# A wider pitch for the rows of X2, two buffers for the k = 0 products, one for the copies of x3, and a new order table

## The chip, the cores and the metric

The kernel runs on one core of a Trainium2 chip. The metric is device time in microseconds (us) of one execution. Times before are the median of three runs; the traces are of one profiled execution. PE is the matrix engine, DVE the vector engine, ACT the scalar engine, POOL the GpSimd engine, SP the engine that issues the DMAs.

## The reference

The input x and the gate logits have 4 batches, 6272 time steps and 256 channels. First comes a gated recurrence over time, then a long convolution over time by FFT, gated by two projections, and an output projection.

```python
f = lower_bound + (1 - lower_bound) * sigmoid(f_logit)
h[t] = f[t] * h[t-1] + (1 - f[t]) * x[t]            # for every batch and channel
x1, x2, x3 = split(h @ w_proj, 3)                   # 256 channels each
x2_conv = irfft(rfft(x2, axis=time) * rfft(filter_fft, axis=time))
out = (x1 * x2_conv * x3) @ w_out
```

## The kernel before, in words

6272 steps are 128 x 49, and the FFT over time is done as matmuls with a transform of length 128 and one of length 49 (98 rows of real and imaginary parts). The work of a batch has these stages, named by the kinds of operations in the order table:

- `load`, `sig`, `u`, `su`, `f`, `scan` (function `hgrn`): 13 chunks of 512 steps are loaded by DMA, ACT takes the sigmoid, POOL the product u, PE transposes, ACT or DVE makes the factor f, and DVE runs the recurrence (L395) into HA, which holds h by channel. Some chunks of the next batch are loaded into X2 while it is free (`lend`).
- `P` and `x2` (`phase_p`): for each of the 49 residues r, two matmuls (L729) with every 49th column of HA give x2 for 128 positions by 256 channels. Residues go in groups of four, the 13th group has one. ACT or DVE copies a group from PSUM into X2 as float16 (L290 on ACT, L295 on DVE). X2 holds 128 rows side by side in a partition, one for each pair of channels, PW elements apart. Within a row, the first channel's 49 values start at element 0 and the second's at element 64; elements 49 to 63 are zero padding (`pads`, L336). A group's copy therefore writes, for each row and each of the two halves, a run of four elements.
- `F1` and `A` (`phase_f1`): a matmul loads 128 elements of X2 from a row's start as weights (L742), so it reads past the row's own 113 elements into the next row's; what comes of those is multiplied by zeros later. The last row needs 16 elements behind it, which are cleared (L339). ACT or DVE copies the results into the part A of HA.
- `mini` and `zm` (`mini`): for each quarter of the rows, the second transform at k = 0 and its product with the filter's spectrum, done by DVE into zp (L763). `slot`, done by POOL, adds two halves of zp into the unit's products PP (L809).
- `F2`, `prod`, `pm`, `I2`, `Th` (`unit`): the second transform, its product with the filter's spectrum (by DVE straight from PSUM, L827, or copied by ACT or DVE and multiplied by POOL, L836), and the first part of the inverse.
- `x13`, `xs`, `z` (`gate`): projections x1 and x3 in 13 chunks and two halves of the channels (L423). ACT or DVE copies x1 to XS. Then either DVE multiplies x3 by it straight out of PSUM (an `xs` on "MUL", L444), or x3 is copied into XS as well and POOL multiplies the two (`z`, L453). The result is zt.
- `I1`, `y`, `proj`, `o`, `store` (`phase_o`): the last part of the inverse (L909), the product with zt on DVE (L915), the output projection (L927), a copy and a DMA to the output.

All of the work is 2430 operations. The string `ORDER` gives, for each in turn, its number, its engine and its PSUM banks, three characters for one operation. `emit` issues them in this order, so it is every engine's order too; engines then wait for each other by semaphores only. "MUL" stands for a product on DVE.

The buffers that the change touches are these:

```python
X2 = konst.tile([128, NEP * PW + 16], F16, name="X2")       # NEP = 128 rows, PW = 113
xv = X2[:, 0:NEP * PW].rearrange("m (i c) -> m i c", c=PW)
zp = konst.tile([128, 2, 2, 2, NA * UE], F16, name="zp")    # one quarter's products at k = 0
XS = konst.tile([128, 4 * XR * Q], F32, name="XS")          # 2 buffers for x1, 2 for x3
```

Of the kernel before, what the change touches and what calls it, by code (L numbers as in the profile page):

```python
# [62 lines left out]
class Plan:  # L63
# [67 lines left out]
    "KD/WEAOCKQCLICRSCSCEpAEBOCPUEHQELSCQEEIICNWCOGCUUCVEESYEMKEJIENKEogETWEUGCMYEqYEzgCaQEcgEVOCbAEXUCYSCfQEYMEZMChWE9gE"
    "0gE+gFIgAGgCTYEKYFRgE1ACZCEeYCcYCgACiOE2YE/ACjYCdSEfQEgIEhIFAYCeCCoUEjWCpECkSEkGClCErUCqQEvSEsECrAElOEwCEtMCxWCvQExK"
    "CyGCwIFTACtUE3WE4OE5OCuEC6SC0QAIYCsYC7CE6UC1AALYCzYAJYAKYAMYE7MDBSDCKE8MC/QFBWFHgFJAFbgB2gCGgFSgCXgFmgFlgFcgDAAFCGFD"
    "OC4SFEQC5CDEUFFAC9SDFEC+CFGIFKYFLWEiYANYC8YEOYDDYFUYDIUDJEDKQFOSDLAFdADRUFMOFNODSEJSQJUADNWFVUDPQFwgFvgB3gFPKFQKFWMD"
    "QIFXMJTSJXTDOGFnAFYWDUQEmYFeYDMYFoYD2YDTYCWgJZDJVCFxADVAFfSFgCDYUFZOFaOFiQDaWFhKDZEFjADbGFpUFqEDhSFkIFsWDdQDiCDfSFrM"
    "FtGJYUJcVFuODGgF5gAHgCHgC3gCngMWgC2gCmgG2gDHgF+gGkgDeADgCEaIECYEyYFyYDcYAOYEuYJasJWYEWYFzQF2WF0ADyADkSJeFMYADlCF1IMX"
    "gMugMigMvgDXgDngDmgG/gGtgDWgJdUJhQJiVD+YF3OF4OJjIGCWGUQGSSJfsGDOGEWJktGQUGRMGTCGVAGFGGISGJCMwAF6YDjYF7YMxYGGQGHIGAUM"
    "kAGBMGWSGYQGOWGXCGPGGZIGMUGNMGKSGLCJmWJnXJrUJtEGcSJoOJpvGaQGeUGgWGdKF8SGbAGhGGfMGlQGnoGiUJsWJwXF9CHISGjMJxQGpoGuUJuG"
    "GysGwsJyHHJCJzAJqYJvYGvYGmYJ0YGxYGoYGqYGzYG3WHKSGrQG5uG7GHLCJ1VJ2XJ6SJ3FGsAJ4vG0UHAQHEoHCoG6YG8YG4YJ8CMZYHDYHBYHFYHO"
    "SG1EHPCHMWJ7UJ/VJ9sG9SHTQHNGHQWKBFHVAG+CKAVKEUKFQHROHGWHcSKGEKHAHSgHXoKCtHHGHbgMjgHkgHtgHlQHpAHgqHeqH2UHfYHWYHhYHdYH"  # L140
# [53 lines left out]
def kernel(  # L194
# [140 lines left out]
    def pads():  # L335
        op("pad", {"POOL": 2.0}, lambda e: nc.gpsimd.memset(xv[:, :, Q:64], 0.0), w=["padX"])  # L336
# [676 lines left out]
```

## Time and profile before

| | |
|---|---|
| median of three runs | 460.8 us (460.41 to 461.16) |
| profiled execution | 461.09 us, its span 459.3 us |
| granted TensorE clock, mean | 0.995 |
| PE busy | 438.5 us (95%) |
| DVE busy | 411.0 us (89%) |
| ACT busy | 403.7 us (88%) |
| POOL busy | 314.8 us (69%) |
| copies into X2 | 29 on ACT, 40.0 us; 23 on DVE, 32.8 us |
| DMA | 119.04 MB, 259 GB/s on average |

The span is from the first to the last instruction of the profiled execution. A row of a group has the line, the engine, the operation, the tiles written and read, the shapes, the count; then, behind the bar, the busy time, the mean time of one in ns, and the idle time of the engine just before them with what ended it. In a timeline the first two numbers are start and length, and a bracket at the end gives idle time before with what ended it.

### The profile page before, as it was taken

Reading aid. Unit: us, or ns where it says so; the run is one execution under the profiler, and the core shown is the slowest. Engines: PE = TensorE matmul, PEld = TensorE weight load, DVE = VectorE, ACT = ScalarE, POOL = GpSimd, SP = SyncE. Lnnn points to the kernel's source line nnn. Section 1 sums busy time; section 2 is a strip of 40 time slices with the busy share of each in tenths; the row PEclk is TensorE's granted clock in tenths of the full one; section 3 lists DMA queues with packets and bytes.
Section 4 is the critical chain, followed back from the end, with each engine's and each line's share of the span. In section 5 each row is a group of like instructions: output and inputs, shape, how many; then the busy total and the mean of one; then the engine's idle time right before and its main releaser. Section 6 shows DMA issues by size and latency. Waiting matters only on the chain.

```text
span 459.3 us, 14538 instructions
## 1 busy us (share of the span) xinstructions
PE 438.5 (95%) x6013; PEld 344.0 (75%) x6013; DVE 411.0 (89%) x458; ACT 403.7 (88%) x549; POOL 314.8 (69%) x290
## 2 busy tenths in 40 slices
PE   8899998999999998999999999999999999999994
PEld 6787877777667878777668888777768886776783
DVE  6989997899999997999999987999999978889972
ACT  7789998999999889999989978999999879998454
POOL 4379993289999553978996926999999503757300
PEclk9999999999999999999999999999999999999998
DMA  8999999467977953588975892688956722663167
GB/s 329 407 398 371 349 344 403 140 231 261 376 266 273 339 199 151 192 269 281 389 273 169 304 358 102 213 262 306 396 193 239 281 80 87 208 194 123 48 258 304
DMA packets 42562, 119.04 MB, mean 259 GB/s; under 512 B 4096, under 2 KB 5760, under 8 KB 42496
## 3 DMA queue, kind: packets, MB, share of 16 engines
q1 hardware_dynamic: 42496, 118.11, 71.3%
q8 instruction: 47, 0.77, 0.6%
q14 instruction: 19, 0.16, 0.1%
HBM read 86.12 MB, written 31.98 MB: 257 GB/s over the span
## 4 chain that ended last, share of the span: by engine, by line
PE 58%; DVE 15%; ACT 11%; issue 6%; POOL 4%; DMA 4%; SPq 1%; ACTq 0%; DVEq 0%; POOLq 0%
PE PS L423 15%; PE PS L846 9%; DVE HA L395 7%; PE PS L927 7%; PE PS L742 6%; PE PS L804 6%; PE PS L374 5%; ACT X L290 5%; PE PS L729 4%; DVE ys L915 3%; PE PS L909 3%; DMA out_dram<-osb 2%; DMA X<-in_moe_filter_fft_dram 2%; PE PS L666 1%; POOL PP L836 1%
## 5 line engine op out<-in xcount | busy, mean ns | idle before, releaser
L395 DVE TENSOR_TENSOR_SCAN HA<-fTs,HA,PS 128x512 f16<-128x512 f32 (+1 forms) x96 | 112.8, 1202 | 1.8 <-ACT fTs L387 0.8
L423 PE MATMUL PS<-HA,W 128*128 128x490 f16 (+1 forms) x416 | 101.6, 368 | 0.9 <-DVE zt L444 0.3
L836 POOL TENSOR_TENSOR PP<-HA,Hu 98x1008 f16<-98x1008 f16 x44 | 92.2, 2105 | 8.4 <-ACT HA L290 4.2
L362 POOL TENSOR_TENSOR XT<-XT,FL 128x1024 f32<-128x1024 f32 (+1 forms) x31 | 67.0, 2165 | 38.4 <-ACT FL L360 38.4
L290 ACT CAST HA<-PS 128x1024 f16<-128x1024 f32 (+1 forms) x107 | 84.0, 817 | 5.3 <-PE PS L742 1.7
L915 DVE TENSOR_TENSOR ys<-PS,zt 128x1024 fp32r<-128x1024 f32 (+1 forms) x52 | 58.4, 1153 | 9.8 <-PE PS L909 4.7
L827 DVE TENSOR_TENSOR PP<-PS,Hu 98x1008 f16<-98x1008 f32 x52 | 61.2, 1199 | 3.6 <-ACT XS L292 0.8
L927 PE MATMUL PS<-Wo,ys 128*128 128x256 f32 x392 | 57.5, 292 | 3.1 <-DVE ys L915 2.1
L387 ACT ACTIVATE fTs<-PS,nomc 128x512 f32<-128x512 f32 (+1 forms) x85 | 55.8, 665 | 4.3 <-DVE HA L395 1.4
L423 PEld LDWEIGHTS <-W 128*128 128x128 f16 x416 | 34.5, 97 | 30.6 <-issue 5.5
L846 PEld LDWEIGHTS <-PP 98*128 98x128 f16 x1024 | 50.0, 97 | 9.5 <-issue 2.2
L444 DVE TENSOR_TENSOR zt<-PS,XS 128x490 f16<-128x490 f32 (+1 forms) x86 | 54.8, 648 | 2.2 <-ACT XS L292 0.8
L362 POOL TENSOR_TENSOR X<-X 128x1024 f32<-128x1024 f32 x21 | 50.0, 2380 | 9.7 <-ACT X L360 7.4
L846 PE MATMUL PS<-FT,PP 98*128 98x98 f16 x1024 | 55.7, 206 | 0.5 <-DVE HA L395 0.5
L292 ACT ACTIVATE XS<-PS 128x490 f32<-128x490 f32 (+1 forms) x86 | 49.5, 585 | 7.2 <-PE PS L423 4.9
L927 PEld LDWEIGHTS PS<-Wo,ys 128*128 128x128 f32 x392 | 49.0, 188 | 8.8 <-DVE ys L915 1.6
L290 ACT CAST Th<-PS 128x784 f16<-128x784 f32 x61 | 49.9, 821 | 3.1 <-PE PS L846 2.6
L729 PE MATMUL PS<-W,HA 128*128 128x256 f16 x392 | 45.5, 273 | 2.3 <-ACT X L290 2.2
L290 ACT CAST X<-PS 128x1024 f16<-128x1024 f32 (+1 forms) x29 | 40.0, 1475 | 8.5 <-PE PS L729 8.5
L729 PEld LDWEIGHTS <-HA 128*128 128x128 f16 x392 | 43.2, 142 | 4.1 <-issue 3.3
L453 POOL TENSOR_TENSOR zt<-XS 128x490 f16<-128x490 f32 x18 | 22.0, 1228 | 32.1 <-DVE ys L915 19.1
L295 DVE CAST X<-PS 128x1024 f16<-128x1024 f32 (+1 forms) x23 | 32.8, 1453 | 10.7 <-PE PS L729 10.6
(108 smaller groups left out, 785.6 us busy)
## 6 DMA issues: line engine op xcount, KB each, us to landing
Hu<-H SPq DMA_DIRECT2D x39, 512.0 KB, 4.7
FL<-in_f_logit_dram SPq DMA_DIRECT2D x27, 512.0 KB, 6.3
XT<-in_x_dram SPq DMA_DIRECT2D x27, 512.0 KB, 7.2
out_dram<-osb SPq DMA_DIRECT2D x24, 512.0 KB, 4.6
X<-in_f_logit_dram SPq DMA_DIRECT2D x21, 512.0 KB, 7.8
X<-in_x_dram SPq DMA_DIRECT2D x21, 512.0 KB, 7.7
out_dram<-PP SPq DMA_DIRECT2D x16, 512.0 KB, 4.5
Hl<-H SPq DMA_DIRECT2D x13, 512.0 KB, 5.2
```

Source lines behind the costliest of these rows:

```text
L290: nc.scalar.copy(dst, src)
L362: op("u", {"POOL": 0.1 + 0.553 * nb}, lambda e, xt=xt, ft=ft: nc.gpsimd.tensor_tensor(xt, xt, ft, op=AOP.mult), r=[("ft", k)], w=[("xt", k)])
L387: nc.scalar.activation(fT, sT, AF.Identity, scale=by, bias=1.0)
L395: nc.vector.tensor_tensor_scan(h, fT, bank(pb)[:, 512 - hn:512 + hn], init, op0=AOP.mult, op1=AOP.add),
L423: nc.tensor.matmul(PS[:, p, 0:n], W13[:, kh, js], HA[:, HB[kh] + t0:HB[kh] + t0 + n], start=(kh == 0), stop=(kh == 1))
L444: nc.vector.tensor_tensor(zd(), px, xs(0), op=AOP.mult)
L729: nc.tensor.matmul(pp[:, r - r0, :], column(HB[kh], q_of(r)), W2[:, kh, :], start=(kh == 0), stop=(kh == 1))
L827: nc.vector.tensor_tensor(pr, px.unsqueeze(1).broadcast_to([TB, 2, UE, 63]), hh(), op=AOP.mult)
L836: nc.gpsimd.tensor_tensor(pr, spec[:, o, :, 1:64].unsqueeze(1).broadcast_to([TB, 2, UE, 63]), hh(), op=AOP.mult)
L846: nc.tensor.matmul(PS[:, ib + o, pr * TB:(pr + 1) * TB], PP[:TB, k, o, n, 2 * pr:2 * pr + 2, :], v[:TB], start=(n == 0), stop=(n == 1))
L915: nc.vector.tensor_tensor(late["ys"][:, yk, :, 0:rn * 128], PS[:, cb:cb + 2, 0:rn * 128], late["zt"][:].rearrange("p k r m -> p k (r m)") ...
L927: nc.tensor.matmul(po[:, i, :], late["ys"][:, yk, kh, i * 128:(i + 1) * 128], Wo[:, kh, :], start=(kh == 0), stop=(kh == 1))
```

## The change

- `PW` goes from 113 to 116: the rows of X2 start 232 bytes apart and not 226, and X2 has 384 elements more in each partition. The elements 113 to 115 of every row are cleared by one more memset on POOL in `tails`, once a batch.
- `zp` has two buffers; quarters use them in turn.
- XS has two buffers for x1 and one for x3, where it had two of each. A copy of x3 now waits for the product `z` of the copy before it.
- The order table is new throughout. It has the same 2430 operations; some sit on another engine. Counted by kind: copies into X2, 31 on ACT and 21 on DVE (before 29 and 23); `xs`, 99 on ACT, 28 on DVE and 81 direct products (before 104, 18 and 86), so POOL multiplies 23 times in `z` and not 18; `o`, 49 on ACT and 3 on DVE (before 52 and 0); `f`, 87 on ACT and 17 on DVE (before 85 and 19). Direct products of units stay 74.

```diff
-PW = 113
+PW = 116
 PF = 113
...
 ORDER = (
-    "A4gA0gBAgA8gBIgAAYAPYA5AAzAAiQAdQAkQAbQAcQAeQAgQAhQABIACIAWYADIAQIATIA6QA1YAfSApSAjSARAAXAAVYA7AASABBIBCSBDCAmUA2UAY"
...
+    "AAYA4gBAgAiQAPYACIA0gADIAQIBIgA8gAdQBEgAkQBQgBMgAbQA5YAcQA6QA1IDogBYgBUgAeSBBYAgSBggAhSARAATYBCSAzAABIAfUBcgA2UApWA7"
...
-    zp = konst.tile([128, 2, 2, 2, NA * UE], F16, name="zp")
+    zp = konst.tile([128, 2, 2, 2, 2, NA * UE], F16, name="zp")
...
-    XS = konst.tile([128, 4 * XR * Q], F32, name="XS")
-    late = {k: XS[:, 2 * i * XR * Q:2 * (i + 1) * XR * Q].rearrange("p (j n) -> p j n", j=2)
-            for i, k in enumerate(("x1s", "x3s"))}
+    XS = konst.tile([128, 3, XR * Q], F32, name="XS")
+    late = {}
...
         def tails(e):
+            nc.gpsimd.memset(xv[:, :, 113:PW], 0.0)
             nc.gpsimd.memset(X2[:, NEP * PW:], 0.0)
...
-                    return late["x3s" if i else "x1s"][:, j, 0:n].rearrange("p (r m) -> p r m", r=Q)
+                    return XS[:, 2 if i else j, 0:n].rearrange("p (r m) -> p r m", r=Q)
...
                 op("xs", dict(either(n), MUL=0.07 + n / 960.0), x3_out,
                    r=["cz", ("x1s", j, 0)] if direct else [],
-                   w=[("z", jb, c) if direct else ("x1s", j, 1)], src=x13[1])
+                   w=[("z", jb, c) if direct else "x3s"], src=x13[1])
...
                 op("z", {"POOL": 0.06 + 2.3 * n / 1000}, z_out,
-                   r=[] if direct else ["cz", ("x1s", j, 0), ("x1s", j, 1)], w=[("z", jb, c)])
+                   r=[] if direct else ["cz", ("x1s", j, 0), "x3s"], w=[("z", jb, c)])
...
             nc.vector.tensor_tensor(
-                zp[:TB],
+                zp[:TB, q % 2],
...
-        op("zm", {"DVE": 0.58}, prod, r=["Hm"], w=["zp"], src=mm)
+        op("zm", {"DVE": 0.58}, prod, r=["Hm"], w=[("zp", q % 2)], src=mm)
...
         op("slot", {"POOL": 0.2}, lambda e: nc.gpsimd.tensor_tensor(
-            PP[:TB, k, :, :, :, 0], zp[:TB, :, :, 0, ka:ka + UE],
-            zp[:TB, :, :, 1, ka:ka + UE], op=AOP.add),
-           r=["zp", "D1"], w=[("Pz", k, 0), ("Pz", k, 1)])
+            PP[:TB, k, :, :, :, 0], zp[:TB, u // NA % 2, :, :, 0, ka:ka + UE],
+            zp[:TB, u // NA % 2, :, :, 1, ka:ka + UE], op=AOP.add),
+           r=[("zp", u // NA % 2), "D1"], w=[("Pz", k, 0), ("Pz", k, 1)])
```

More of the change, by code (lines that the diff above doesn't have):

```diff
@@ L131 @@
[L131 to L140, printed above, removed]
@@ new lines @@
+    "IBDCAWYAXYA9IA+WAjQBkgAmQA3MBFIDrgDpgBJYBKQDsgBGSBLAAsUAoUEDgDqgAtUD3gAxUBNYA/OBRIBSUAlQArQAUIBHKAEgBTEASABOQAZSBVYA"
+    "aCD4gBPAAnTAvTAYIBZIBaUBbMAqTAVYBhYAyTBWSBXCEbgBdIAuQBiQEEgBjIBeUAwSBlYBfEEPgDtABmSBnKBvUBqSBwEBoQEQgDuYBrKBxUBpIB6S"
+    "EngEcgByMEFABtQB0UBsYBuAAFYBzYB7KDvWB1MD5AB4SB/QB5CDzUCAAB8YDwODxOD6YCBSEzgAGgD0ECKQCCCD1MB9WEdACESB+GCLICDYEGYD7UCF"
+    "KCIQD8ECRWD/SCJAD9MERACPQCMYE9gEogEAKCSGESYCNUCQAEHWELQE0gFHgEBKCOECaSEMAFIgEeYEIOEJOCbCEpAE+gENICUUCYSETWCZCCVECdSE"
+    "KYCTYEXQCeCAJYEUOEVOChUEYACiME1ACfSEfWEZICcYAIYEWYCoUCgCEgOE/ACqQCpMEqYCjYEjSCrAEhOCkUFbgFSgEkCFRgCxQCvWClECHgElKFJA"
@@ new lines @@
+    "CwGE2YAKYCsYCGgB3gErUCyICtSEsMEtMEvQCuCC6WEwAC0SEiYC7GE3UExIC1CC4WE4ME6QC5GFdAE5MC9WFAYFlgFcgCzYC8YAMYDISC+GE7IE8IDB"
+    "UFmgC3gAHgDJCFBWC/SFCOFDOFKYFEQDCEFTAC2gALYDACCWgDKUFFACngFvgDESDLEFGIFLWDDYDFCDNUDMYFUYFwgB2gDHgDPQDOEFOSFMOFNODQAJ"
+    "SUFnAFeYFVQFPKFQKDRWJUEFWAFYUDSGFXIDaSFZEFoYFfWDbCFaMJTQFgGFiSJVAFhODUUF5gCmgCXgMWgDGgFjCAOYFpQDVEANYDTYFkKDhWFxAFqA"
+    "D2YEuYJXUDiOFsSJZEFrIDYWFtCEmYFyYMigDfUF+gDZGFuKFzQDgEDdWEOYF0AF2UMjgEyAECAGkgMXgMugF1IDkSEaYDyYDcYD+YF3MJYQDlCJcRF4"
+    "MGQUGRMDeGJWYJaAF6YJbYF7YDmgGMSGUWJeJGNKDngG2gMvgMYAGVGGSUGCQGYSGDAGZCGTMGOWGKUDWgMkAGPOMlYDjYMZYGEQGIWGWSGLEGGUGJOG"
@@ new lines @@
+    "XKGFAMwAGHMGAWJdQJhRGBGJfAJiSG/gGtgDXgJjJJkqGcWGdGGgUJgYGhEGaQGbIJmSGeWMxYJnTGfGF8UJoKGlQJpLF9EJrSGuWGpoJqYGiUJtCGyG"
+    "JsTGjMJwRJxXGnoJuDHIUGmYJyBGoYGzYGqYGvYHJEG3SGwuHSgHbgGrQG5CGsAJzvGxYHAUG4YJvYG7qG0WHOQG1GJ0YG6YHBYG8YHCsJ1TJ2SHPAHK"
+    "WJ3LJ6UHLGHEsHMQJ7THNAG9WJ8MHkgHtgJ9rJ4CHTUHQQJ/SKATHDYJ5YHFYG+GHXEHRIHVsHGQKBCHcWHHAHWYKCrHlUHguHeuHnEJ+YKESKFTKGCH"
+    "UYHdYKJUHYYHhYIAgKHDH2QHZSHfYKIYH3AKLMHiWIJgHaCHpsHqYHoYHmYHuQHyoKDYHwoHjGKKUH8SKMEH4WH6UHzYH9CHvYKNYHxYKORH7EHrSISg"
+    "H5OIbgKQBIBUHsCH+WIFsMaQIDEIKSMbAIEYH/OMeUIOCMcIH0WM6gMfEKPTH1GMgMIkQICYIPYILYITWIlAIGYM7gIugKRrIcUIXGIMqIHQKSYIeEKT"
@@ new lines @@
+    "XIIAINYIYYIUYJlYIgMKVHIVuMmSMqQMnCIQUNGgMrAIWYMoKNHgIZWIREI3gJAgMsIIaGIvUM8AKUSIoWIzsIfYIhYI0YIdYIpGKYTImQKWqKZVInAI"
+    "qWIxsKXYKdSMVgNTgKaDIyYM9YIiQNSgIrOKfCKeTIjAKgrKbtMyWIsQNIAI4SMzGItIKhYM2UNJYI6CKiQKjRM0OM3EKnSNegJJgM4MM+WORgNfgKkA"
+    "I8CIwYKpCKoQKlpKqoKrYI7YKcYI9YKmYI5YM/GNCUNogNpgKsRNDENAOI1SKuBKtQKxRI2CNEMNUAJBWNKSKvoKzBI+UNVYJFuNLCNOQJDGNMKJGYI/"
+    "EKyXK2WNPAK0vK1YJCYNWUNaSK4GNQINXEK3WK7XNgAK5uJKQF/gU6gNygU5gOagJLYJEYKwYK9HNYMNhYK8WJMANzgLAXJHULBQK+uNbCLCHJOoJIEN"
+    "iWLFRLGULKVLDoNjGNcKLHBLLQLIEJNYLMNNRYNlSNqANkOK/YLJYJPYLPRN8gJQUNmCN9gOQgLNoLOYNrYLQWR1XR2QLRBNnKJRER4AR3HLUULSuLZS"
@@ new lines @@
+    "N0AK6YN1YM5YNNYM1YNZYLTYMdYLEYLVMNsQNvWLaKNtALWUObgOGgOHgNwGNuILbSLXENxOLjQLcCLeULkIN+AN2WN5SNFYN/YMhYN3GOcAN6CLfMLl"
+    "QN4OLgULmAN7KLoWLhELtQOIALpOLdgLngLYgLigOASODUOBCOJYLuILqWOEEOSAOCKLvQLrGOFML3SLwALyWL4KOKUONQLzOL5SOOAOLEOPIL0WL6CM"
+    "tYMpYOTYOMML8QL1GOUSOXWL9IOVCR6UVGgOkgNdYOlYOdYNBYVFgOYGOWKR8EU7AOZOL+QU8YOeUOfEOhSOgMMBWOiCL/AMGUOjKMCOMHML2gVRgL7g"
+    "LxgO7SO3QO9WOrUO8KMAgLsgO+OO4AOsEO/SOtQO1WOnUOuAO2OOoMPACVHAOvQO5SOwAOxWO6CVTAOzQOyGO0AOpSMDUOqKOmYVIYMLWMEEPBQMMOPF"
+    "SPCAMFgVSgPDUPGKMIWPEEMQSMJGPLQMRKPHUPPoPNoR5YR7SPIEMNWR9CPJUMOGPTSPKMP1gPbQPXqPQYPMYPVqPOYPUYPrUPfAPRWPsER/TPcYPgYP"
@@ new lines @@
+    "YYPWYPSGPjUPdoP+gQHgSASSBDPZWPlESCqPvQPaGPnsPoYPmYPeYPhSPwAPtWPiKP2UPuGPxQPkYR+YPpSPyAP6sP4sP5YPqCP/WU9QMPgMKgPzSQDu"
+    "QQgQjgQBGSEUSFVSJWSKXU+AP0KSGEU/IQZSSLGQEYQCYP7YP3YQAYQaCSOUSPWSHtVBQSRGSMvQISSQEMSWP8UMTGVCIVDIQKCQFWP9EQMqQNYQJYQL"
+    "YSNYSSYSTSQGGQRUSVCQfQQVsQTsQUYSUTQgAQbWSYSQcGQdQSZVSdUVUYQWYQSYSWrQeAQsgVdgSaKQOWMUgQ+gSfESbtQhSQkQQPGQiKQtUVfAQXSQ"
+    "vEQuYScYQmoQooQlYSeWQYCSguQwYSiQSjUSkAShYVJSQpYQ1gRRgVegQxEQ2QSlsVKCVNWQ6IQyYQnYQ4AQqUVLKVOGVVQQrEVPORHSVWAQzUVpgRIC"
+    "VXIQ/WVqgRagQ0ERNSRBuSnQROCQ3YSmYQ7YSXYQ5YRJUSoRRDuSpARCYSsWRKERLSSuOStQREYRAYRjgU4gRMCQ8UVgYSqpWBgSvoV2gRSWQ9EV1gRP"
@@ new lines @@
+    "SVZQRWuRUGRFUVaARVYRQKRGEVbIVhWVrAViOVjORkSSxUSyVRTYRXYRmCRYQVsYSrYSzERoCS2SS3US4CS0tRbWRZAVlSS5sRfuW9gS7VS8UTAQWDAR"
+    "dGS9NS+sRcYWLgWCgRsgTCAS1YRlYRgYRnYRpYSDYSIYVmCTBXTDvTEYTFRTGVTKUTHBVnKV3ATLQTPRVtWVxSTItTMEV4YVuGTNoRqUSwYdcgWzgTRB"
+    "VvOVyCRrETQQTURVzKReYS6YTOYV5WTWBV9UV6GTSoRtSV7OWMgW+gWVgTVRRxCTJYWWgTTYWEYTZQTaTddgTbATXpRhWV+ETcrRiGV/MTYYTeRTgBTf"
+    "QThoTiYTjTTkWToRTpXW/ATlDRvqRyYS/YRwYTmuTqBWFUTdYV0YRuYTnYTrHTtTWGETsYRzQTvDWHMTuSR0ATyTTzWT0DTwqT3QWNAWIUTxYT8ST1uT"
+    "2YT4IVEYWAYVcYaYWWXAWJEaZXWfgW0gWggT9KWKMT5QabHaaGUBSWOYWYYT6AWPWUCKWSUWQGT+QWpgWTEWROWqgUGST/AWZWUHKUDQUAgWhAWiYVwY"
@@ new lines @@
+    "WUMWaGUISUEAWbOULUVYYUJCWcQUQWUMMUVSWdAUROUFgT7gUNUWrAWeIUSWUOEWsYXAYVQYVAYUWKUaQUTGUbIWjUWmSWtWWkEWnCWlMUcQW1AWoKUX"
+    "UWuGUdAWvOUfSUYEUgKWwQW2YW3WXHgUKgWxAW6UW4GWyIUhSW5OdogW7EXBQUiCW8MV8YVkYVoYVMYXIYXJYUkWXCAXESd0gUegUPgXDIUpUadQXFCd"
+    "pgUZgUUgXGKUlOUqMafAXMSXaQXYWXbIUmUXOQdeAdqAXNCUnMXPAXQSUogUjgXWUXgQXRCXZOd2AXhAXXMXSSXUUXiQXTCXKWXLGXVEXjIXcSdrYdfY"
+    "XeQXdKUuWUzUXfAUrSUvOXmQUsCU0MXqWXnIacYXrGXkUXoSXpCaeQXlMUwWagoXsSXuUUxGXtKXysXwEahYXvYdgQX2SXxYaiWajUX4CX6qakGdhAal"
+    "sX7YanSaoVasTaqFapKdkWXzYX5YYYgauDdiIeAgYhgd1gYOUdlGX0SYPEdmOdsQX3YamYX1CX+UarYdtIYGWX/YYCEX8SYAsYKGYDYatVaxXayUX9CY"
```

74 lines of the change are left out of this document (22 added, 52 removed).

## The prediction

> **What bounds the kernel now.** I read the page's head and busy line first, then a table of windows around each stage that fills X2, then timelines of PE, ScalarE (ACT) and VectorE (DVE) in those stages, then groups kept apart by shape, and last the waits of GpSimd (POOL).
>
> ```profile
> span 459.3 us, 14538 instructions
> ...
> PE 438.5 (95%) x6013; PEld 344.0 (75%) x6013; DVE 411.0 (89%) x458; ACT 403.7 (88%) x549; POOL 314.8 (69%) x290
> ```
>
> PE, DVE and ACT are all near full, so no engine is the bound by its share alone, and one has to look at stages. I cut four windows, each from the first projection matmul into X2 (L729) to the first F1 matmul that reads X2 (L742), and add one stretch of the steady work behind them.
>
> ```profile
> 72.00:86.30 14.30, 12.90 (x106) 11.38 (x105) 10.93 (x11) 12.40 (x11) 3.65 (x4) 1.00 0.91 336
> 167.80:182.00 14.20, 12.82 (x127) 12.35 (x124) 11.02 (x8) 12.50 (x11) 2.38 (x1) 1.00 0.62 218
> 267.60:282.50 14.90, 14.39 (x138) 13.31 (x134) 11.98 (x10) 12.51 (x12) 4.81 (x3) 1.00 0.74 293
> 367.90:382.30 14.40, 13.07 (x115) 11.95 (x111) 9.17 (x7) 11.31 (x10) 0.00 (x0) 1.00 0.14 53
> ...
> 282.50:320.00 37.50, 37.14 (x562) 27.95 (x563) 35.56 (x42) 35.00 (x51) 34.29 (x28) 1.00 0.69 227
> ```
>
> The columns are length, then busy time of PE, PEld, DVE, ACT, POOL, and the granted clock, which is 1.00 throughout. The four X2 stages take 14.3 + 14.2 + 14.9 + 14.4 = 57.8 us. In them PE has gaps, which it hardly has in the steady stretch (37.14 of 37.50). What ends the gaps stands in PE's timeline.
>
> ```profile
> 84.93 1.40 PE L423 MATMUL PS<-HA,W 128*128 128x490 f16 x6 [0.27 <-ACT X L290]
> ...
> 167.82 11.09 PE L729 MATMUL PS<-W,HA 128*128 128x256 f16 x98
> 178.81 1.21 PE L927 MATMUL PS<-Wo,ys 128*128 128x256 f32 x8
> 181.40 0.63 PE L909 MATMUL PS<-ID,Th 64*128 64x128 f16 x16 [1.38 <-ACT X L290]
> ...
> 280.31 0.74 PE L909 MATMUL PS<-ID,Th 64*128 64x128 f16 x20
> ...
> 382.06 0.29 PE L909 MATMUL PS<-ID,Th 64*128 64x128 f16 x4
> ```
>
> In batch 1 the 98 matmuls run without a stop in 11.09 us, and then PE stands 1.38 us until ACT's last copy into X2. In the other batches the stops lie inside the stage. The releaser is a copy into X2 each time: the copies (13 in a batch, shared by ACT and DVE) are late, not the matmuls.
>
> **The pitch of 116, the first term.** A row group's copy writes, for each of 128 rows and each of two halves, a run of four float16 (8 bytes). At a pitch of 113 elements the runs start 226 bytes apart, so every second one starts off a 4-byte word; at 116 it is 232 bytes, and with halves 128 bytes apart and groups 8 bytes apart each run fills exactly one 8-byte word. What that is worth is bounded by these groups.
>
> ```profile
> L290 ACT CAST HA<-PS 128x1024 f16<-128x1024 f32 x56 | 55.7, 1020 | 3.2 <-PE PS L742 1.7 <-PE PS L758 0.4 <-issue 0.2
> ...
> L290 ACT CAST Th<-PS 128x784 f16<-128x784 f32 x61 | 49.9, 821 | 3.1 <-PE PS L846 2.6
> ...
> L290 ACT CAST X<-PS 128x1024 f16<-128x1024 f32 x28 | 38.8, 1479 | 8.5 <-PE PS L729 8.5
> ...
> L360 ACT ACTIVATE FL<-FL 128x1024 f32<-128x1024 f32 x27 | 28.9, 1076 | 0.0
> ...
> L295 DVE CAST X<-PS 128x1024 f16<-128x1024 f32 x20 | 28.9, 1468 | 10.5 <-PE PS L729 10.4
> ...
> L295 DVE CAST HA<-PS 128x1024 f16<-128x1024 f32 x8 | 9.5, 1220 | 1.4 <-PE PS L742 0.8 <-issue 0.6
> ...
> L290 ACT CAST f<-PS 128x1024 fp32r<-128x1024 f32 x6 | 6.8, 1162 | 2.8 <-PE PS L651 2.8
> ...
> L295 DVE CAST X<-PS 128x256 f16<-128x256 f32 x3 | 4.1, 1352 | 0.2 <-PE PS L729 0.2
> ...
> L295 DVE CAST Th<-PS 128x784 f16<-128x784 f32 x3 | 2.9, 965 | 0.0
> ...
> L290 ACT CAST X<-PS 128x256 f16<-128x256 f32 x1 | 1.4, 1377 | 0.0
> ```
>
> Contiguous float16 from PSUM (HA) costs 1020 ns on ACT and 1220 on DVE for 1024 elements; X of the same size costs 1479 and 1468. The last group of a batch writes runs of one element, a quarter of the data, and costs 1377 and 1352: the price hangs on the runs, not on the elements. Two rows tell what part of a run it is. Th also writes runs of four float16 from a strided PSUM read, but its runs start on 8-byte words, and its 784 elements take 821 and 965 ns: 1.05 and 1.23 ns an element, no dearer than HA's 1.00 and 1.19. The filter's own copy (f) reads PSUM in the same order as X does and still takes 1162 ns on ACT. So neither short runs nor the read is the cause; half-filled words are what is left. I take HA's 1020 and 1220 for the new copies, with 1162 and the old 1479 as the other bounds on ACT and the old 1468 on DVE. The last group of a batch keeps its price, since one element never fills a word.
>
> A copy's pitch in a queue is a little under its duration, and this sets the stage:
>
> ```profile
> 371.79 4.02 DVE L295 CAST X<-PS 128x1024 f16<-128x1024 f32 x3
> ...
> 374.16 8.02 ACT L290 CAST X<-PS 128x1024 f16<-128x1024 f32 x6 [1.34 <-PE PS L729]
> ...
> 183.04 2.84 ACT L290 CAST HA<-PS 128x1024 f16<-128x1024 f32 x3
> ...
> 383.03 2.36 DVE L295 CAST HA<-PS 128x1024 f16<-128x1024 f32 x2 [0.21 <-PE PS L742]
> ```
>
> That is 1.34 us for X on either engine against 0.95 and 1.18 for HA. In the new order table, ACT has 6, 8, 8 and 9 of the 13 copies of batches 0 to 3 (before 7, 7, 7 and 8). With eight at 0.95 and the next batch's three sigmoids at 1.08, ACT needs 10.8 us, less than the 11.09 of the matmuls: the stage becomes PE's. Its length is then the matmuls plus what PE has between them and the first F1. The new table keeps nearly the same such work: three gate projections in batch 0 (1.40), one output projection and an inverse in batch 1 (1.21 + 0.63), two projections and two inverses in batch 2 (1.21 + 1.21 + 0.74), one and a short one in batch 3 (1.21 + 0.29). The last copy (1.02) hides behind these where they are longer, and I add 0.1 to 0.2 for handing over. So 12.7, 13.0, 14.4 and 12.7, together 52.8: 5.0 us less than 57.8. This term is the forecast's whole gain. If PE's filler work fits in gaps elsewhere, each stage is 11.1 + 1.02 + 0.2 = 12.3 and the term is 8.6; if the copies keep their price it is nothing or a loss.
>
> [...]
>
> **The other edits.** Their rows:
>
> ```profile
> L453 POOL TENSOR_TENSOR zt<-XS 128x490 f16<-128x490 f32 x18 | 22.0, 1228 | 32.1 <-DVE ys L915 19.1 <-ACT XS L290 11.5 <-ACT XS L292 1.0
> ...
> L836 POOL TENSOR_TENSOR PP<-HA,Hu 98x1008 f16<-98x1008 f16 x44 | 92.2, 2105 | 8.4 <-ACT HA L290 4.2 <-POOL PP L809 1.8 <-POOL XT L362 1.0
> ...
> L336 POOL MEMSET X<- 128x1920 f16 x4 | 7.3, 1823 | 0.7 <-PE PS L374 0.7
> ```
>
> ```profile
> POOL XT L362 <- ACT FL L360: 38.4, 10, 11.5
> ...
> POOL PP L809 <- DVE zp L763: 7.8, 3, 3.0
> ...
> DVE zp L763 <- PE PS L758: 2.9, 5, 0.9
> ```
>
> ```profile
> L444 DVE TENSOR_TENSOR zt<-PS,XS 128x490 f16<-128x490 f32 x78 | 50.6, 657 | 1.8 <-ACT XS L292 0.7
> ...
> L292 ACT ACTIVATE XS<-PS 128x490 f32<-128x490 f32 x81 | 47.1, 590 | 7.0 <-PE PS L423 4.7 <-DVE zt L444 1.2 <-DVE PP L827 0.5
> ...
> L297 DVE TENSOR_SCALAR XS<-PS 128x490 f32<-128x490 f32 x15 | 9.9, 662 | 1.0 <-PE PS L423 0.8
> ```
>
> - The added memset fills 128 runs of three elements, four times. By L336 (0.95 ns an element) it is 0.4 us; if each run costs what a run of one element costs X (1377 over 256 is 5.4 ns), 0.7. That is 1.6 to 2.8 us of POOL in all, ahead of the next u or z in its queue. POOL stands 38.4 us waiting for sigmoids, which covers it: nothing. Without that cover it is 0.4 to 0.7 a batch.
> - Two buffers of zp let DVE write a quarter's products before POOL has read the last ones. DVE's waits at zp are for PE (2.9), never for POOL, so this opens no wait that the trace has: nothing. Since POOL waits 7.8 us for zp, an earlier product could help by that at most; POOL has slack, and I keep 1 us for the low end.
> - One buffer for the copies of x3: each copy that isn't multiplied at once must wait until POOL's product z of the one before is done. I counted the new table: 23 such copies (18 before), 20 of them on ACT. Most follow the z before by 16 to over 100 of 2430 entries (0.19 us of span each). Five are closer, by 1, 4, 9, 12 and 13. For the first I charge one z, 1.2 us, on ACT at the start of batch 0's X2 stage; behind it in ACT's queue stand a sigmoid and that stage's copies. The other way, ACT gives five XS copies away (5 x 0.59 = 3.0 us less), so I take the two together at nothing, bounds -1.8 and the rival below.
> - DVE takes over ten XS copies (6.6 us more) and five products fewer (3.3 less). Most of these lie in batches 0 and 3. I take nothing and keep 3.3 as a bound.
>
> The rest of the order table changes neighbours, not totals. Sum: the profiled execution took 461.1 us (span 459.3 and 1.8 around it); 461.1 - 5.0 = 456.1. The median before is 0.3 below the profiled time, so 455.8.
>
> **Rivals.**
> - *More than the stages.* Filler finds room elsewhere: -8.6 and -1 give 451.5, less 0.3: 451.2. For it: ACT gets some 11 us lighter in copies. Against: PE is 99% busy in the steady stretch. Chance 0.15.
> - *Given back.* DVE, 95% busy in the steady stretch, carries 3.3 us more there, and the 1.2 us wait isn't covered: 461.1 - 5.0 + 4.5 - 0.3 = 460.3, no change. Chance 0.07.
> - *The x3 buffer holds the queue* (slower). At the five close places ACT or DVE stands behind POOL, which has a product (2.105) ahead of z (1.228): 3.3 us each, 16.7, less the distance in the table (39 entries, 7.4 us) and the 5.0 gained: 461.1 + 4.3 - 0.3 = 465.1. It decides from the point where these waits sum to over 5.0 us. For it: POOL is 34.29 of 37.50 busy in the steady stretch, and at four of the five places the new table has a product or a u right ahead of z. Against: POOL alone would have to run late, and it is POOL that waits for ACT's sigmoids now (38.4 us). Chance 0.12.
> - *The copies stay at 1.48 us.* The new order gives ACT one copy more in each of batches 1, 2 and 3; where ACT isn't hidden, as in 2 and 3, 2 x 1.34 = 2.7: 463.8 - 0.3 = 463.5. Against it stands Th. [...] Chance 0.08.
>
> **The numbers.** The forecast has 0.58. A measurement of this kernel can tell about 0.2%, 0.9 us, from no change. Faster: 0.58 + 0.15 = 0.73; same 0.07; slower 0.12 + 0.08 = 0.20. The range reaches from the lowest case (451) to that of unchanged copies (464); the x3 rival lies outside with the edges. For the faster cases alone it is 451 to 459.
>
> **What would show it.** The 1024-element copies into X at 1020 to 1162 ns on ACT and 1220 on DVE, with the 256-element ones unchanged; the four X2 stages at 12.5 to 14.5 us; no wait of PE's L729 on an X copy over 0.3 us. Wrong: X at 1.4 us or more; or fast copies and a span that isn't shorter, with waits of XS on zt (L453) on ACT or DVE, or XT and u on POOL moved behind the scans.

## The result, and the profile after

The changed kernel takes 461.61 us (median of 22 runs, 460.71 to 462.76), the kernel before 460.44 us on the same chips (22 runs, 460.08 to 461.52). The ratio is 1.0022, with a 95% interval of 1.0014 to 1.0030: about as large as the smallest difference that can be told, and on the slower side. 455.8 us had been forecast. The profiled execution took 461.1 us, its span is 459.3 us, like that of before.

The page's busy line of the changed kernel:

```profile
PE 439.4 (96%) x6013; PEld 346.3 (75%) x6013; DVE 411.8 (90%) x458; ACT 389.0 (85%) x539; POOL 326.0 (71%) x308
```

ACT lost 14.7 us of work, as it should, and the end did not move. The groups kept apart by shape, for what writes X2:

```profile
L289 ACT CAST X<-PS 128x1024 f16<-128x1024 f32 x28 | 27.6, 1042 | 8.7 <-PE PS L729 8.5
L294 DVE CAST X<-PS 128x1024 f16<-128x1024 f32 x20 | 23.9, 1219 | 13.0 <-PE PS L729 11.6 <-DMA FL<-in_f_logit_dram 1.4
...
L289 ACT CAST X<-PS 128x256 f16<-128x256 f32 x3 | 4.1, 1352 | 0.0
...
L338 POOL MEMSET X<- 128x384 f16 x4 | 2.7, 682 | 0.0
```

The copies fell to 1042 and 1219 ns, the prices forecast from HA and Th, and the copies of runs of one element kept theirs. Next the windows of the four X2 stages, cut as before from the first L729 to the first L742 (length; busy PE, PEld, DVE, ACT, POOL; granted clock; DMA):

```profile
72.60:84.60 12.00, 12.00 (x106) 11.20 (x105) 8.96 (x9) 10.68 (x13) 8.02 (x8) 1.00 1.03 393
167.90:180.50 12.60, 12.42 (x125) 12.12 (x123) 8.06 (x8) 10.10 (x12) 3.81 (x4) 1.00 0.71 283
265.90:279.40 13.50, 13.50 (x135) 13.14 (x133) 10.42 (x9) 10.93 (x12) 4.72 (x2) 1.00 0.81 307
369.10:381.30 12.20, 12.16 (x115) 11.86 (x112) 6.98 (x7) 9.16 (x11) 0.00 (x0) 1.00 0.23 92
```

They take 50.3 us where they took 57.8, and PE is busy for 50.1 of them: 7.5 us are gained. (Before, the first L729 started at 72.16 us and not at the window's 72.00; from there it is 57.6, and 7.3 gained.) All of it is lost outside the stages. The stretches between them, and the one behind the last, in the kernel before:

```profile
86.30:167.80 81.50, 79.51 (x1267) 60.48 (x1266) 79.02 (x82) 76.83 (x114) 69.36 (x59) 1.00 0.73 260
182.00:267.60 85.60, 84.53 (x1296) 63.94 (x1294) 81.90 (x90) 81.17 (x119) 72.24 (x59) 1.00 0.76 262
282.50:367.90 85.40, 84.47 (x1306) 64.66 (x1306) 82.11 (x91) 78.86 (x115) 75.75 (x62) 1.00 0.72 256
382.30:459.30 77.00, 69.67 (x930) 52.82 (x928) 60.63 (x70) 54.73 (x76) 31.75 (x31) 0.97 0.51 182
```

and in the changed kernel:

```profile
84.60:167.90 83.30, 81.53 (x1272) 61.61 (x1271) 80.47 (x87) 77.56 (x114) 73.11 (x62) 1.00 0.71 256
180.50:265.90 85.40, 84.12 (x1295) 64.11 (x1296) 83.13 (x91) 79.13 (x115) 68.06 (x59) 1.00 0.73 259
279.40:369.10 89.70, 85.08 (x1308) 65.83 (x1306) 87.16 (x94) 79.03 (x115) 72.24 (x60) 0.98 0.69 246
381.30:459.30 78.00, 70.24 (x930) 53.11 (x930) 62.49 (x75) 53.59 (x72) 37.72 (x35) 0.99 0.50 180
```

The first is 1.8 us longer, the third 4.3, the last 1.0, and the start before the first stage some 0.4. In the third PE has 4.6 us without work where it had 0.9, and its granted clock is under 1.00. The timeline there, all engines:

```profile
317.97 2.36 POOL L362 TENSOR_TENSOR XT<-XT,FL 128x1024 f32<-128x1024 f32 x1
...
319.10 3.88 DVE L294 COPY HA<-HA 128x512 f16<-128x512 f16 x1
...
320.28 0.34 POOL L809 TENSOR_TENSOR PP<-zp 98x32 f16<-98x32 f16 x1
...
320.49 2.35 POOL L362 TENSOR_TENSOR XT<-XT,FL 128x1024 f32<-128x1024 f32 x1
...
322.79 2.15 POOL L836 TENSOR_TENSOR PP<-HA,Hu 98x1008 f16<-98x1008 f16 x1
...
324.39 0.69 PE L374 MATMUL PS<-idc,FL 64*128 64x64 f32 x8 [3.60 <-DVE zt L444]
...
325.44 1.49 PE L846 MATMUL PS<-FT,PP 98*128 98x98 f16 x16
```

One copy on DVE takes 3.88 us. It is a `wrap`: 512 columns of HA are copied behind the end of the row, for the projections into X2 that read across it. The kernel before has 46 of its 48 on POOL; the new table puts this one, of batch 3, on DVE. It ends just after POOL's second u, at 322.98 us for 322.84. PE, which waits for DVE's next product with x1 (L444), stands 3.60 us. And then PE is slow: 16 matmuls of L846 take 1.49 us, where those at 330.89 take 0.88. Windows of 2 us show its clock (the number behind POOL's):

```profile
320.00:322.00 2.00, 0.79 (x16) 0.50 (x12) 2.00 (x1) 1.42 (x3) 2.00 (x3) 1.00 1.04 383
322.00:324.00 2.00, 0.00 (x0) 0.00 (x0) 1.90 (x3) 0.00 (x0) 2.00 (x2) 1.00 1.04 424
324.00:326.00 2.00, 1.61 (x24) 1.50 (x25) 1.77 (x3) 0.46 (x1) 1.02 (x2) 0.58 1.01 408
326.00:328.00 2.00, 2.00 (x30) 1.66 (x29) 1.37 (x2) 1.10 (x3) 0.25 (x1) 0.57 1.03 397
328.00:330.00 2.00, 2.00 (x40) 1.53 (x37) 1.96 (x2) 2.00 (x5) 1.34 (x1) 1.00 1.02 395
```

The 0.58 and 0.57 are means over the change: in windows of 0.25 us the clock is 0.50 from 324.3 to 327.7 us, for 3.4 us.

### The profile page after: what moved, and what is told of

Same layout as the page of the kernel before. It is cut to its first block, busy times and chain, and to the rows that moved or that the text cites. A ratio compares the mean times of both kernels' runs of the same rounds, so it can differ in the third digit from the quotient of the medians.

```text
span 459.3 us, 14550 instructions
## 1 busy us (share of the span) xinstructions
PE 439.4 (96%) x6013; PEld 346.3 (75%) x6013; DVE 411.8 (90%) x458; ACT 389.0 (85%) x539; POOL 326.0 (71%) x308
## 4 chain that ended last, share of the span: by engine, by line
PE 66%; DVE 19%; issue 6%; ACT 6%; POOL 2%; DMA 1%; DVEq 0%; ACTq 0%; POOLq 0%
PE PS L423 15%; PE PS L846 9%; PE PS L729 8%; DVE HA L395 8%; PE PS L374 7%; PE PS L804 6%; PE PS L927 6%; PE PS L742 6%; DVE ys L915 5%; DVE zt L444 3%; PE PS L909 3%; PE PS L666 2%; ACT X L289 1%; PE PS L618 1%; PE PS L651 1%
## 5 line engine op out<-in xcount | busy, mean ns | idle before, releaser
L836 POOL TENSOR_TENSOR PP<-HA,Hu 98x1008 f16<-98x1008 f16 x46 | 96.3, 2104 | 8.7 <-issue 7.0
L289 ACT CAST HA<-PS 98x512 f16<-98x512 f32 (+1 forms) x107 | 84.7, 819 | 5.6 <-PE PS L804 1.5
L387 ACT ACTIVATE fTs<-PS,nomc 128x512 f32<-128x512 f32 (+1 forms) x87 | 57.2, 666 | 10.0 <-PE PS L374 6.1
L827 DVE TENSOR_TENSOR PP<-PS,Hu 98x1008 f16<-98x1008 f32 x50 | 59.0, 1198 | 1.5 <-PE PS L804 0.5
L846 PEld LDWEIGHTS <-PP 98*128 98x128 f16 x1024 | 50.2, 98 | 10.9 <-issue 2.6
L846 PE MATMUL PS<-FT,PP 98*128 98x98 f16 x1024 | 56.2, 207 | 0.5 <-POOL PP L809 0.2
L444 DVE TENSOR_TENSOR zt<-PS,XS 128x490 f16<-128x490 f32 (+1 forms) x81 | 51.1, 648 | 4.4 <-PE PS L423 1.6
L291 ACT ACTIVATE XS<-PS 128x490 f32<-128x490 f32 (+1 forms) x79 | 45.3, 583 | 4.1 <-PE PS L423 3.1
L453 POOL TENSOR_TENSOR zt<-XS 128x490 f16<-128x490 f32 (+1 forms) x23 | 25.9, 1128 | 29.7 <-DVE ys L915 23.5
L729 PE MATMUL PS<-W,HA 128*128 128x256 f16 x392 | 43.8, 273 | 0.0
L729 PEld LDWEIGHTS <-HA 128*128 128x128 f16 x392 | 42.9, 142 | 0.6
L742 PEld LDWEIGHTS <-X 128*128 128x128 f16 x512 | 31.5, 98 | 9.3 <-issue 2.8
L294 DVE CAST X<-PS 128x1024 f16<-128x1024 f32 (+1 forms) x21 | 25.2, 1224 | 14.7 <-PE PS L729 13.3
```

Of the source, the lines that this page charges most:

```text
L289: nc.scalar.copy(dst, src)
L444: nc.vector.tensor_tensor(zd(), px, xs(0), op=AOP.mult)
L729: nc.tensor.matmul(pp[:, r - r0, :], column(HB[kh], q_of(r)), W2[:, kh, :], start=(kh == 0), stop=(kh == 1))
L742: nc.tensor.matmul(pa[:, i, :], X2[:, j:j + 128], D1, start=True, stop=True)
L827: nc.vector.tensor_tensor(pr, px.unsqueeze(1).broadcast_to([TB, 2, UE, 63]), hh(), op=AOP.mult)
L836: nc.gpsimd.tensor_tensor(pr, spec[:, o, :, 1:64].unsqueeze(1).broadcast_to([TB, 2, UE, 63]), hh(), op=AOP.mult)
```

## The experiments

Theory A: the pitch brings what the stages show, and the new order table takes it back, most of it by this one copy. Rival B: what the stages save is lost in the full stretches behind them, with any table. A kernel's ratio is to the kernel before on the same chip, with its 95% interval.

**The pitch alone, with the old order table.** For room, the two buffers for copies of x3 hold float16.

```diff
-PW = 113
+PW = 116
...
-    XS = konst.tile([128, 4 * XR * Q], F32, name="XS")
-    late = {k: XS[:, 2 * i * XR * Q:2 * (i + 1) * XR * Q].rearrange("p (j n) -> p j n", j=2)
-            for i, k in enumerate(("x1s", "x3s"))}
+    XS = konst.tile([128, 2, XR * Q], F32, name="XS")
+    X3 = konst.tile([128, 2, XR * Q], F16, name="X3")
+    late = {"x1s": XS, "x3s": X3}
...
         def tails(e):
+            nc.gpsimd.memset(xv[:, :, 113:PW], 0.0)
```

> The kernel before with its own order table, and only the pitch of X2 at 116 with the memset for it. To make room, the two buffers for copies of x3 hold float16 (18 products of POOL read them). Theory A, the new order table gives back what the pitch brings: with the old table the four X2 stages go from 57.6 us to about 51 and this reaches the end, so 454 to 457 us. Rival B, whatever the X2 stages save is lost in the full stretches behind them with any table: 459.5 us or more. Under both, copies into X2 at 1.02 to 1.05 us on ACT and 1.22 on DVE.

452.63 us, ratio 0.9819 (0.9806 to 0.9833), the fastest here together with the pitch of 114 below. Copies by shape, and the sum line of the windows of its four X2 stages:

```profile
L290 ACT CAST X<-PS 128x1024 f16<-128x1024 f32 x28 | 27.1, 1023 | 11.6 <-PE PS L730 11.6
L295 DVE CAST X<-PS 128x1024 f16<-128x1024 f32 x20 | 24.1, 1221 | 10.5 <-PE PS L730 10.3
```

```profile
sum 50.30, PE 50.24 PEld 48.46 DVE 37.76 ACT 37.60 POOL 11.02; mean PE 12.56 PEld 12.12 DVE 9.44 ACT 9.40 POOL 2.76
```

The stages are as short as in the changed kernel, and here the gain reaches the end, and more: 8.2 us, which is below theory A's range of times. Rival B falls.

**The new order table alone**, at the old pitch:

```diff
-PW = 116
+PW = 113
...
-            nc.gpsimd.memset(xv[:, :, 113:PW], 0.0)
```

> The changed kernel with the pitch back at 113 and without the added memset; new order table, buffers as changed. Theory A: the pitch is worth 5 to 7 us in the X2 stages, so this takes 466 to 469 us against 461.6 for the changed kernel. Rival B: the pitch is worth nothing at the end, 461 to 463 us.

470.29 us, ratio 1.0202 (1.0188 to 1.0216), a little above theory A's range. Copies and the stages' sum:

```profile
L289 ACT CAST X<-PS 128x1024 f16<-128x1024 f32 x28 | 39.4, 1488 | 5.9 <-PE PS L728 5.8
```

```profile
sum 58.50, PE 53.12 PEld 48.95 DVE 40.59 ACT 52.28 POOL 16.15; mean PE 13.28 PEld 12.24 DVE 10.15 ACT 13.07 POOL 4.04
```

So the change is two changes: some 8 to 9 us less by the pitch, some 9 more by the rest.

**The slow copy on ACT.** In the order table of the changed kernel, the `wrap` with number 1919 goes from DVE to ACT, at the same place.

> The changed kernel with one of its 2430 operations on another engine: the copy of 512 columns of HA in batch 3's recurrence that took 3.88 us on DVE in the trace (others of its kind take 0.6 to 0.7) goes to ACT, at the same place of the order. Theory A: that copy stood for about 3.2 us behind POOL's products, held DVE's queue and PE, and is most of what the stretch between the X2 stages of batches 2 and 3 lost (4.3 us): now 457 to 459 us, and that stretch 3 to 4 us shorter. Rival B: the stall covers another wait that comes next, as for loads: 460.5 us or more.

455.28 us, ratio 0.9876 (0.9860 to 0.9891): 6.3 us less than the changed kernel, more than expected. Its timeline has

```profile
319.82 0.62 ACT L287 COPY HA<-HA 128x512 f16<-128x512 f16 x1
```

and the third stretch between the stages is

```profile
279.10:364.10 85.00, 83.89 (x1308) 64.86 (x1306) 83.06 (x93) 79.14 (x116) 71.91 (x60) 1.00 0.71 259
```

85.0 instead of 89.7 us. ACT starts the copy at 319.8, so its data and its place were free by then; it was DVE that couldn't do it. The rest of the 5.9 us between the two spans lies mostly in the last stretch (77.1 for 78.0), where no operation differs; why stays open.

**The same copy with two sources**, on DVE in its first place:

```diff
-                   lambda e, a=t0, z=z, o=HB[kh]: copy(
-                       e, HA[:, o + S + a:o + S + z], HA[:, o + a:o + z]),
+                   lambda e, a=t0, z=z, o=HB[kh]: nc.vector.tensor_tensor(
+                       HA[:, o + S + a:o + S + z], HA[:, o + a:o + z], HA[:, o + a:o + z], op=AOP.max)
+                   if e == "DVE" else copy(
+                       e, HA[:, o + S + a:o + S + z], HA[:, o + a:o + z]),
```

> The changed kernel with that same copy left on DVE at the same place, but done as the maximum of the columns with themselves, an operation with two sources. Theory A: the plain copy between two places of SBUF waits for POOL, which works without a break beside it, because such a copy needs something that POOL holds; an operation with two sources does not need it: 0.4 to 0.7 us, and 457 to 459 us in all. Rival B: it waits for its data or for a place to write, whatever the operation: again 3 us or more, 461 us or more.

461.64 us, ratio 1.0019 (1.0009 to 1.0028):

```profile
318.92 4.02 DVE L405 TENSOR_TENSOR HA<-HA 128x512 f16<-128x512 f16 x1
```

I was wrong about what the copy needs: with two operands from SBUF it waits just as long. The rival's reason (data or place) doesn't hold either, since ACT could do it. What both forms have in common is that they work from SBUF to SBUF, beside POOL.

**Later on DVE, beside POOL's float16 products; later still, beside a u; and in the middle of a product.** Number 1919 stays on DVE, behind the unit's product at entry 1797 of the table, behind the product with x1 at 1833, and behind the scan at 1807, in the order in which these ran.

> The changed kernel with the slow copy left on VectorE as it is, but five of VectorE's operations later (behind a unit's product and before two scans), where GpSimd does products of two float16 tiles (L836) in a row and no u. Theory C, only GpSimd's products of float32 tiles (u, z) keep the copy out: it takes 0.2 to 0.7 us, and the kernel 455 to 456 us. Theory A, any work of GpSimd without a break keeps it out: 3 us or more, and 458 us or more.

> The changed kernel with the slow copy left on VectorE, but later still, where GpSimd begins a single u of 2.4 us with a float16 product behind it. Theories A and C both have it wait for that u: 1.5 to 2.5 us under C, 4 us or more under A, since GpSimd's work goes on without a break. Rival B, the stall belongs to the data or to the place in the first position: 0.2 to 0.7 us. In all 456 to 458 us under C.

456.26 us (ratio 0.9899, 0.9885 to 0.9914) and 458.91 us (0.9956, 0.9939 to 0.9973). The first one's timelines of DVE and of POOL:

```profile
324.72 0.28 DVE L292 COPY HA<-HA 128x512 f16<-128x512 f16 x1
```

```profile
322.55 2.13 POOL L834 TENSOR_TENSOR PP<-HA,Hu 98x1008 f16<-98x1008 f16 x1
324.62 0.58 POOL L807 TENSOR_TENSOR PP<-zp 98x32 f16<-98x32 f16 x1
```

and the second one's:

```profile
329.11 2.55 DVE L292 COPY HA<-HA 128x512 f16<-128x512 f16 x1
```

```profile
329.16 2.35 POOL L360 TENSOR_TENSOR XT<-XT,FL 128x1024 f32<-128x1024 f32 x1
```

In the first the copy takes 0.28 us. POOL's small sum began 0.10 us ahead of it and did not keep it out; it was the sum that grew, from 0.34 to 0.58. The kernel still takes 1.0 us more than with the copy on ACT, and what of the later place costs that is open. In the second, beside a u, the copy takes until just behind that u's end. Its total is above the 456 to 458 us of theory C. In its profile PE stood 1.97 us, from 330.9 to 332.9, until the scan behind the copy was done, and half a microsecond after PE worked again its clock fell too:

```profile
332.00:334.00 2.00, 1.09 (x4) 0.29 (x3) 2.00 (x3) 0.48 (x2) 2.00 (x4) 0.86 0.28 99
334.00:336.00 2.00, 2.00 (x32) 1.63 (x32) 1.76 (x3) 1.04 (x3) 2.00 (x2) 0.50 0.01 4
336.00:338.00 2.00, 2.00 (x16) 0.92 (x12) 1.50 (x2) 1.74 (x4) 0.64 (x2) 0.79 0.00 0
```

The copy's two times fit theory C, that only float32 products keep it out, but in the first kernel the copy came up at a product's very end. Hence the third:

> The changed kernel with the slow copy on VectorE placed one scan later than where it took 0.28 us, so that it comes up in the middle of a float16 product on GpSimd (about 325.8 us, product from 325.1 to 327.1) and not at the end of one. Theory C, only products of float32 tiles keep it out: 0.2 to 0.4 us, 455.5 to 456.5 us in all. Theory D, any operation of GpSimd keeps it out until its end and only the moment was lucky: 1.3 to 1.6 us, 456.5 to 458 us.

457.51 us, ratio 0.9934 (0.9922 to 0.9945):

```profile
325.85 1.48 DVE L292 COPY HA<-HA 128x512 f16<-128x512 f16 x1
```

```profile
325.08 2.10 POOL L834 TENSOR_TENSOR PP<-HA,Hu 98x1008 f16<-98x1008 f16 x1
327.14 0.39 POOL L807 TENSOR_TENSOR PP<-zp 98x32 f16<-98x32 f16 x1
```

Theory C falls, and here D's figures hold: beside a float16 product the copy took 1.48 us, until just behind its end at 327.2. In the five profiles with such a stall whose timelines of DVE and POOL stand in this document, the plain copy ends 0.14 to 0.15 us behind the end of a u, a z or a product. No run took POOL's work away from beside it; that POOL is the cause rests on these ends, on ACT's copy and on the moves. What of POOL's holds the copy up, no run shows. Two things stay open: the 0.28 us beside a sum that had begun, which doesn't fit theory D, and that the copy in its first place let two ends of POOL's operations pass (320.3 and 320.6 us) and got in only at the third, at 322.8.

**The same stall in the old order table.** In the kernel with the pitch alone, one `wrap` of batch 3 (number 1895) goes from POOL to DVE, behind the scan at entry 1743.

> The kernel with the old order table and the new pitch (452.6 us), with one copy of 512 columns of HA in batch 3's recurrence moved from GpSimd to VectorE, behind the scan that ends at 315.8 us, where GpSimd does two float32 u in a row from 315.2 to 319.8. If such a copy waits for u in any table, it takes 4.0 to 4.4 us, the stretch between the X2 stages of batches 2 and 3 grows by 3 to 4.5 us, and the whole is 456 to 457 us. If the loss was peculiar to the new table, 0.2 to 0.7 us and 452 to 453 us.

459.29 us, ratio 0.9944 (0.9919 to 0.9969), against 452.63: one copy costs 6.7 us in the median. Timelines of DVE and of POOL, and windows of 2 us:

```profile
315.21 4.41 DVE L293 COPY HA<-HA 128x512 f16<-128x512 f16 x1
```

```profile
314.82 4.65 POOL L361 TENSOR_TENSOR XT<-XT,FL 128x1024 f32<-128x1024 f32 x2
```

```profile
318.00:320.00 2.00, 0.00 (x0) 0.00 (x0) 2.00 (x2) 0.00 (x0) 1.47 (x1) 0.82 1.03 381
320.00:322.00 2.00, 1.75 (x18) 1.49 (x18) 1.90 (x3) 0.25 (x1) 0.00 (x0) 0.50 1.07 426
322.00:324.00 2.00, 2.00 (x6) 0.52 (x4) 1.28 (x2) 0.56 (x1) 0.00 (x0) 0.50 1.02 416
324.00:326.00 2.00, 2.00 (x21) 1.11 (x20) 0.69 (x3) 1.17 (x2) 0.07 (x1) 0.50 1.03 412
```

The stall is the forecast one, its price at the end is more: PE stood 4.17 us, and the granted clock is 0.50 for 6.8 us, from 319.3 to 326.1 (worked out from the means of 0.82 above and of 0.97 from 326 to 328, as steps between 1.00 and 0.50). Three of the 11 executions took 455.1 to 455.3 us, at a mean granted clock of 0.996 to 0.998, the others 458.9 to 459.7 at 0.990 or 0.991. So in the executions with the higher mean clock the stall costs 2.6 us, less than its length, and in the others about 4 more; by an estimate from the profile, 6.8 us at half the clock are worth 3.4. The time at 0.50 was 3.4 us in the changed kernel and is twice that here. The wait of 1.97 us above was followed by 3.4 us at 0.50 as well (worked out likewise from its 0.86, 0.50 and 0.79), the wait of 1.38 us in the kernel before (at 181.40) by 1.00. What lies between these two was not tried, and what sets the length of the time at 0.50 stays open.

**The two buffers.** From the kernel with the slow copy on ACT, once with two buffers for copies of x3 again (float16), once with one buffer of zp:

```diff
...
-    XS = konst.tile([128, 3, XR * Q], F32, name="XS")
+    XS = konst.tile([128, 2, XR * Q], F32, name="XS")
+    X3 = konst.tile([128, 2, XR * Q], F16, name="X3")
...
-                   w=[("z", jb, c) if direct else "x3s"], src=x13[1])
+                   w=[("z", jb, c) if direct else ("x3s", j)], src=x13[1])
...
```

```diff
-    zp = konst.tile([128, 2, 2, 2, 2, NA * UE], F16, name="zp")
+    zp = konst.tile([128, 2, 2, 2, NA * UE], F16, name="zp")
...
```

> The changed kernel with the slow copy on ACT (455.3 us), and two buffers for the copies of x3 again (in float16, for room). What is left against the old table with the new pitch is 2.6 us, 2.5 of it between the X2 stages of batches 0 and 1. Theory A, the single buffer of x3 costs that: 452.5 to 453.5 us. Rival B, the single buffer costs nothing and the rest lies in the order itself: 455 to 455.6 us.

> The changed kernel with the slow copy on ACT (455.3 us), and one buffer of zp again. Theory: the second buffer is worth nothing or nearly so, since no wait of VectorE for GpSimd at zp stands in any trace: 455 to 456 us. Rival: the new order relies on it, products at k = 0 then wait for GpSimd's sums and hold VectorE: 457 us or more.

455.33 us (ratio 0.9877, 0.9860 to 0.9894) and 455.59 us (0.9884, 0.9868 to 0.9901), against 455.28: the single buffer of x3 costs nothing, the second of zp brings 0.3 us at the most, within the intervals nothing.

**What of the pitch it is, and a control.** The kernel with the pitch alone at 114, and at 113 with the float16 buffers only:

```diff
-PW = 116
+PW = 114
```

> The kernel with the old order table and the new pitch (452.6 us), but a pitch of 114: every run of four float16 then starts on a 4-byte word, and every second one off an 8-byte word. Theory 4, half-filled 4-byte words are the price: copies into X2 at 1.02 to 1.05 us on ACT and 1.22 on VectorE as with 116, and 452 to 453 us. Theory 8, runs that reach over an 8-byte border are the price: about 1.25 us on ACT, 1.35 on VectorE, and 455 to 458 us.

> The kernel before, pitch 113 and old order, with nothing changed but the two buffers for copies of x3 in float16, as in the run with the pitch alone. If that run's gain is the pitch's, this is the kernel before within 0.3%: 459.5 to 461.5 us. If the float16 buffers bring part of it, it is 458 us or less.

452.68 us (ratio 0.9827, 0.9814 to 0.9839) and 460.63 us (1.0006, 0.9993 to 1.0020). At 114:

```profile
L290 ACT CAST X<-PS 128x1024 f16<-128x1024 f32 x28 | 27.8, 1057 | 11.2 <-PE PS L730 11.2
L295 DVE CAST X<-PS 128x1024 f16<-128x1024 f32 x20 | 24.1, 1222 | 10.5 <-PE PS L730 10.3
```

Theory 4 holds: with every run on a 4-byte word, every second one still off an 8-byte word, ACT's copies take 1057 ns for 1023 at 116 and DVE's 1222 for 1221. The float16 buffers do nothing for the time.

## Why the prediction was wrong, point by point

- *Copies into X2 at HA's price:* right, 1042 and 1219 ns for 1020 and 1220. Th and the one-element copies were the rows to read. I had ascribed the whole price to half-filled words; 114, at 1057 and 1222 ns, bears it out.
- *The stages end at PE's work:* right, but mis-sized: 5.0 us forecast, 7.5 measured (7.3 from the first L729). I added up PE's durations and something for handing over, and they overlap: in batch 0 of the changed kernel F1 starts 12.0 us after the first projection, where I had 12.7. The table's filler work stayed, as assumed.
- *"The rest of the order table changes neighbours, not totals":* the step that failed. I counted the operations that changed engine by kind and priced them by their usual durations, and by engine the count of `wrap` hardly differs: 46 on POOL, one on DVE and one on ACT before, 45, one and two after. But the one on DVE is another, in batch 3 and beside other work of POOL. So a term was put at nothing by totals, where the neighbours set the price: 3.88 us in place, and 6.3 us at the end (the changed kernel against the one with that copy on ACT). The kernel before had a sample: its one `wrap` on DVE took 0.69 us, until just behind the end of a z of POOL, where 0.28 was the shortest time.

```profile
69.60 0.69 DVE L295 COPY HA<-HA 128x512 f16<-128x512 f16 x1
```

```profile
68.92 1.23 POOL L453 TENSOR_TENSOR zt<-XS 128x490 f16<-128x490 f32 x1 [0.30 <-PE PS L666]
```

- *The clock:* the four windows and the steady stretch showed 1.00, and I took the price of a wait on PE to be its length. In the changed kernel the clock was 0.50 for 3.4 us behind the wait of 3.60, and the executions of the old order table with the lower mean clock took about 4 us more than those with the higher.
- *The x3 buffer holds the queue:* no. No wait of XS for POOL's z stands among the changed kernel's long waits, and giving the buffer back changes nothing. That the change came out slower is not by this rival. *Given back:* the outcome is this one's, with a chance of 0.07, and its mechanism isn't: DVE's ten more copies of XS are not shown to have taken it. That 461.6 us lies in the range of 451 to 464 is luck: the upper end stood for copies that stay slow, and they became fast.
- *zp and the memset at nothing:* right; the memset is 0.68 us as bounded.
- Of the way from 452.6 (pitch, old table) to 461.6 us, 6.3 are the copy. The other 2.7 lie in the new order: the stretch between the first two X2 stages takes 83.3 us with the copy on ACT as well, and 80.7 with the old table. By the tables, the new one leaves three gate projections more of batch 0 to it, 44 for 41, and has one fewer of batch 1 in it, 3 for 4. That was counted and not tried, so the cause of the 2.7 us stays open.

## What to carry to other kernels

Try a pitch at which every run of 16-bit results starts on a 4-byte word: one pad element a row did it here and took 29% off ACT's copies (1479 to 1057 ns) and 17% off DVE's (1468 to 1222). When work is moved between engines, price it beside its neighbours in time, not by its mean: a copy within SBUF that fits on DVE in 0.28 us took up to 4.41 us beside POOL's u. And a wait on PE can cost more than its length: here the granted clock was 0.50 for 3.4 us behind waits of 1.97 and 3.60 us and for 6.8 us with one of 4.17, in a kernel where 8 of 11 executions had the lower mean clock. So a profile's clock row belongs beside every such gap.

## What the runs showed of the hardware that was not expected

- Float16 copies from PSUM into X2, 1024 elements in runs of four, took 1479 ns on ACT and 1468 on DVE at a pitch of 113, with every second run off a 4-byte word, and 1057 and 1222 at 114 and 1023 and 1221 at 116, with none. That half-filled words are the price is my reading of these.
- DVE's maximum of two float16 operands in SBUF took 4.02 us in the place where the plain copy took 3.88, and ended 0.28 us behind POOL's second u.
- POOL's sum of 32 columns grew from 0.34 to 0.58 us beside the copy of 0.28: in this one case it went the other way.
- After PE stood 1.97 and 3.60 us the granted clock was 0.50 for 3.4 us each time, and with a wait of 4.17 us for 6.8. The fall did not come at one fixed point: with the 4.17 us it came while PE still stood, with the 1.97 us 0.5 us after PE worked again. In the copy with two sources PE stood 3.73 us; behind it the first eight matmuls of L374 took 0.46 us, where they took 0.69 at 0.50 in the changed kernel, and the 16 of L848 that began 0.65 us after PE worked again took 1.12, where 16 such had taken 0.87 before the wait.
